# Copying the second operand of a split product with two strided transfers per pair instead of five, and swapping the high and low halves

## The chip, the cores and the metric

The kernel runs on one core of one Trainium2 chip. The metric is the device time of one execution in microseconds (us), the median over executions. Everything below that is called a span is the time from the first to the last instruction of one profiled execution; the time of an execution is a little longer than its span.

## The reference

Two stages follow each other. The first is an attention through 49 agents, for 4 batches of 12800 rows of 128 channels; the second is a gated causal convolution with 5 taps and two 128 x 128 weights.

```python
scale = 1.0 / np.sqrt(q.shape[-1])
def sm(a, b):
    s = scale * (a @ b.transpose(0, 2, 1))
    s = s - s.max(-1, keepdims=True)
    e = np.exp(s)
    return e / (e.sum(-1, keepdims=True) + 1e-09)
agent_v = sm(agents, k) @ v            # (4, 49, 128)
x = sm(q, agents) @ agent_v            # (4, 12800, 128)
xp = np.concatenate([np.zeros((B, 4, D)), x], axis=1)
gate_pre = sum(conv_w[k] * xp[:, k:k + S, :] for k in range(5))
gate = 1.0 / (1.0 + np.exp(-gate_pre))
return (gate * (x @ w_val)) @ w_out
```

## The kernel before

x is never formed. It is the product of 49 softmax weights per row with 49 vectors per batch, so the convolution and the value product are taken on the 49 weights directly, with weights folded once per batch: for each tap, and for the value, a 49 x 128 matrix.

**Split products.** Softmax weights and folded weights are each kept as a high and a low half in 16 bits. Of the product (high + low) x (high + low) three parts are kept: high x high, low x high, and high x low. The tile x1 holds, for every row of the sequence (in its columns), 128 partitions: the 49 high halves (0 to 48), the 49 low halves (49 to 97), and the first 30 of the high halves once more (98 to 127, NDUP = 30). Against it stand the folded weights: high, high again, and the low halves of the first 30. For the remaining 19 of the high x low products there is no room in 128 partitions, so a second tile, x2, takes them: it holds high rows 29 to 48 of x1 (20 rows, X2R = 20) five times over, shifted by 0 to 4 columns, one copy for each tap, in 100 partitions. One matmul over x2 then adds the missing part for all five taps.

**Units and pairs.** A batch has 10 units of 1280 rows. For every unit the scores of the queries are taken on TensorE, a softmax follows on DVE, POOL and ACT, and the weights are split into the tile pt (ACT writes the high half at L713, POOL the second copy of 30 at L718 and the low half at L726). pt is then turned into x1: for the first four units by ten transposes on TensorE (L757) and two copies (ACT L764, DVE L769), afterwards by one transposing transfer on the SP queue (L743). When a pair of units is in x1, `shifts` issues the copies into x2 (L791): five transfers, one for each tap, each of 20 partitions; for the first four units this is done for each unit by itself, and of the first unit's five transfers two are issued from ACT's queue.

**Chunks.** The convolution goes over 100 chunks of 512 columns. Each chunk takes five matmuls over x1 (L828, one for each tap) and one over x2 (L832) into the gate, a tanh on ACT (L841), one matmul over x1 (L855) and one over x2 (L859) into the value, a product on DVE (L868), a split into two 16-bit halves (ACT L874, POOL L879), three output matmuls (L898, L899, L900), a copy on ACT (L912) and, for every second chunk, a store on the SP queue (L927). The output matmuls of a chunk are placed two chunks behind its gate matmuls. In between stand the scores of later queries (L363), the keys of the next batch and its agent values (L463).

**Folding the weights.** Once per batch `fold_weights` makes the folded weights: normalisation and scales on DVE (L506 to L528), high halves (L563, L568), copies of these on ACT (L579, L583), low halves by `rest` (instructions at L548: two for the value, two for the gates), then eight transposes on TensorE (L593), and the same for the output weights (L613 to L662).

**Order.** All steps are given to a planner (`Plan`) with an estimated duration each. It keeps TensorE's steps in the order in which they were given, and orders the steps of DVE, ACT, POOL and the SP queue by the length of what depends on them, using the estimates. A step that issues a transfer carries its issue time and its time on the wire. Every engine then runs its own list in order, and waits where something is missing.

Of the kernel before, what the change touches and what calls it, by code (L numbers as in the profile page):

```python
# [13 lines left out]
ALU = mybir.AluOpType  # L14
# [8 lines left out]
UNIT = 1280  # L23
# [4 lines left out]
TAPS = 5  # L28
HALO = TAPS - 1
PAD = 16  # L30
NDUP = 30
X2LO = 29
X2R = 20


NLOAD = 11
# [135 lines left out]
def tile_agent_attention_gated_conv(  # L172
# [9 lines left out]
    nc = tc.nc  # L182
    B, C, N = qT.shape
    A = 49
# [31 lines left out]
    x1 = const.tile([P, PAD + N], F16, name="x1")  # L216
# [27 lines left out]
    def bank():  # L244
# [16 lines left out]
        out=fold, in0=ident[:, 0:AP_], in1=ident[:, AP_:P], op=ALU.add  # L261
# [217 lines left out]
    gw = const.tile([P, TAPS, A], F32, name="gw")  # L479
# [5 lines left out]
    def fold_weights(b):  # L485
        x = b % 2
        wst, unscale, oscale = wst_sb[x], unscales[x], oscales[x]
        stat, wo16 = stats[x], wo16s[x]
        dve = nc.vector
        pt, at_t = small(b)  # L490
# [14 lines left out]
        def normalise():  # L505
# [8 lines left out]
                out=gw, in0=avT.unsqueeze(1).to_broadcast([P, TAPS, A]),  # L514
                in1=conv_sb.unsqueeze(2).to_broadcast([P, TAPS, A]), op=ALU.mult,
# [4 lines left out]
        def gate_scale():  # L520
# [12 lines left out]
        pv = pv_  # L533
# [3 lines left out]
                out=pv[:, 0:A], lhsT=wval_sb, rhs=avT, start=True, stop=True  # L537
            ),
            ["avT", "moe"], [at_v], key="m",
        )  # L540
        x2g = wst[:, TAPS + 1, 0 : TAPS * X2R].rearrange("p (k r) -> p k r", k=TAPS)
        x2v = wst[:, TAPS + 2, 0 : TAPS * X2R].rearrange("p (k r) -> p k r", k=TAPS)
        ghi = wst[:, 0:TAPS, 0:A]
        vhi = wst[:, TAPS, 0:A]
        off = NDUP - X2LO

        def rest(out, full, s, hi):
            dve.scalar_tensor_tensor(  # L548
                out=out, in0=full, scalar=rs[:, s : s + 1], in1=hi,
                op0=ALU.mult, op1=ALU.subtract,  # L550
            )

        def val_weights():
            dve.tensor_reduce(
                out=mx[:, 1:2], in_=pv[:, 0:A], axis=AX.X, op=ALU.max,
                apply_absolute_value=True,
            )
            dve.tensor_scalar(
                out=mx[:, 1:2], in0=mx[:, 1:2], scalar1=TINY, scalar2=1.0 / WS,
                op0=ALU.max, op1=ALU.mult,  # L560
            )
            dve.reciprocal(out=rs[:, 1:2], in_=mx[:, 1:2])
            dve.tensor_scalar_mul(vhi, pv[:, 0:A], rs[:, 1:2])  # L563
            rest(wst[:, TAPS, 2 * A :], pv[:, 0:NDUP], 1, vhi[:, 0:NDUP])
            rest(x2v[:, HALO, off:], pv[:, NDUP:A], 1, vhi[:, NDUP:])

        def gate_weights():
            dve.tensor_scalar_mul(ghi, gw, rs[:, 0:1])  # L568

        def gate_rest():  # L570
            rest(wst[:, 0:TAPS, 2 * A :], gw[:, :, 0:NDUP], 0, ghi[:, :, 0:NDUP])
            rest(x2g[:, :, off:], gw[:, :, NDUP:], 0, ghi[:, :, NDUP:])

        w_ = ("wst", x)
        add("dve", 0.4, gate_weights, ["gw", "rsg"], [(*w_, "g")])
# [36 lines left out]
        def unscales_():  # L612
# [6 lines left out]
                out=wo, in0=wout_sb, scalar1=unscale[:, 1:2], scalar2=1.0,  # L619
# [47 lines left out]
    def queries(b, u):  # L667
        g = b * NU + u
        x = g % 2
        i = slot_of["q", b, u]  # L670
        ps, at = bank()
        sT, d, e, w, r, sm = sts[x], qw[g % 3], qw[g % 3], qw[g % 3], qr[x], qsm[x]
        pt = pts[g % 3]
        sa = sT[:, :, 0:A]
        add("pe", 1.07, lambda: score_matmuls(b, ld[i], ps), [("ld", i)], [at], key="sc")
        add("dve", 0.84, lambda: transpose_blocks(sT, ps[:, :, 0:GT]), [at], [("sT", x)])
        add(
            "dve", 0.62,
            lambda: nc.vector.tensor_reduce(out=qmx[x], in_=sa, axis=AX.X, op=ALU.max),  # L679
            [("sT", x)], [("qmx", x)],  # L680
        )
        add(
            "pool", 1.05,
            lambda: nc.gpsimd.tensor_tensor(  # L684
                out=d, in0=sa, in1=qmx[x].unsqueeze(2).to_broadcast([P, NBLK, A]),
                op=ALU.subtract,
            ),
            [("sT", x), ("qmx", x)], [("qw", g % 3)],
        )
        add(  # L690
            "act", 0.6,
            lambda: nc.scalar.activation(out=e, in_=d, func=AF.Exp, scale=SCALE),
            [("qw", g % 3)], [("qw", g % 3)],
        )

        def sums():
            nc.vector.tensor_reduce(out=sm, in_=e, axis=AX.X, op=ALU.add)
            nc.vector.scalar_tensor_tensor(
                out=sm, in0=sm, scalar=1.0 / QS, in1=tiny, op0=ALU.mult, op1=ALU.add
            )  # L700
            nc.vector.reciprocal(out=r, in_=sm)

        add("dve", 0.95, sums, [("qw", g % 3)], [("qr", x)])
        add(
            "dve", 0.68,
            lambda: nc.vector.tensor_tensor(
                out=w, in0=e, in1=r.unsqueeze(2).to_broadcast([P, NBLK, A]), op=ALU.mult
            ),
            [("qw", g % 3), ("qr", x)], [("qw", g % 3)],
        )  # L710
        p_ = ("pt", g % 3)
        add(
            "act", 0.58, lambda: nc.scalar.copy(out=pt[:, :, 0:A], in_=w),  # L713
            [("qw", g % 3)], [(*p_, 0)],
        )
        add(
            "pool", 0.44,
            lambda: nc.gpsimd.tensor_scalar(  # L718
                out=pt[:, :, 2 * A :], in0=w[:, :, 0:NDUP], scalar1=1.0, scalar2=0.0,
                op0=ALU.mult, op1=ALU.add,  # L720
            ),
            [("qw", g % 3)], [(*p_, 2)],
        )
        add(
            "pool", 1.09,
            lambda: nc.gpsimd.tensor_tensor(  # L726
                out=pt[:, :, A : 2 * A], in0=w, in1=pt[:, :, 0:A], op=ALU.subtract
            ),
            [("qw", g % 3), (*p_, 0)], [(*p_, 1)],
        )  # L730
# [43 lines left out]
    def shifts(b, u):  # L774

        g = b * NU + u
        if g >= SINGLE and g % 2 == 0:
            return
        n = 1 if g < SINGLE else 2
        u0 = u + 1 - n  # L780
        s = g // 2
        x2 = x2s[s % 3]
        o = (g + 1 - n) % 2 * UNIT
        src = [(x, v) for v in range(max(u0 - 1, 0), u + 1) for x in ("x1", "x1b")]
        for k in range(TAPS):
            c = PAD - HALO + u0 * UNIT + k

            q, e = (nc.scalar, "act") if g == 0 and k % 2 else (nc.sync, "dma")
            add(
                e, 0.75,  # L790
                lambda k=k, c=c, q=q: q.dma_start(  # L791
                    out=x2[k * X2R : (k + 1) * X2R, o : o + n * UNIT],
                    in_=x1[X2LO : X2LO + X2R, c : c + n * UNIT],
                ),
                src, [("x2", s % 3, o + i * UNIT, k) for i in range(n)], 0.26 * n,
            )


# [4 lines left out]
    def gates(t):  # L803
        b, n0, w = chunks[t]
        x = b % 2
        stat, unscale = stats[x], unscales[x]
        if t < NT:
            banks[t] = gate[:, 0:w], "gate", val[:, 0:w], "val"
        else:
            ps, at = bank()  # L810
            banks[t] = ps[:, 0, 0:w], at, ps[:, 1, 0:w], (*at, 1)
        pg, at_g = banks[t][:2]
        units = sorted({max(n0 - HALO, 0) // UNIT, (n0 + w - 1) // UNIT})
        seg = (b * NU + units[-1]) // 2
        halves = sorted({(b * NU + n // UNIT) % 2 * UNIT for n in (n0, n0 + w - 1)})
        segs_ = sorted({(b * NU + n // UNIT) // 2 for n in (n0, n0 + w - 1)})
        assert len(segs_) == 1
        x2 = x2s[segs_[0] % 3]
        o2 = n0 - (segs_[0] * SEG - b * N)
        xs = [("x1", u) for u in units] + [("x1b", u) for u in units]  # L820
        x2k = [("x2", segs_[0] % 3, h, k) for h in halves for k in range(TAPS)]
        st = [("stat", x, 0), ("stat", x, 1)]
        scale = w / CH

        def matmuls():
            for k in range(TAPS):
                c = PAD - HALO + n0 + k
                nc.tensor.matmul(  # L828
                    out=pg, lhsT=stat[:, k, :], rhs=x1[:, c : c + w],
                    start=(k == 0), stop=False,  # L830
                )
            nc.tensor.matmul(  # L832
                out=pg, lhsT=stat[0 : TAPS * X2R, TAPS + 1, :],
                rhs=x2[0 : TAPS * X2R, o2 : o2 + w], start=False, stop=True,
            )

        th = ths[t % NT_][:, 0:w]
        add("pe", 1.3 * scale, matmuls, xs + x2k + st, [at_g], key="c")
        add(
            "act", 0.16 + 0.46 * scale,  # L840
            lambda: nc.scalar.activation(out=th, in_=pg, func=AF.Tanh, scale=unscale[:, 0:1]),  # L841
            [at_g, ("unscale", x)], [("th", t % NT_)],
        )
        return stat, x2, o2, xs, x2k, st, th
# [117 lines left out]
    for b in range(B):  # L962
        t0 = b * NCH
        for i in range(NU):
            g = b * NU + i + LEAD
# [92 lines left out]
```

## Time and profile before

| | |
|---|---|
| median of 3 runs | 432.69 us (429.56 to 434.14) |
| the profiled execution: time, span | 431.22 us, 429.4 us |
| TensorE (PE) busy | 402.9 us, 94% of the span |
| ACT, DVE, POOL busy | 300.4, 297.0, 224.3 us |
| granted TensorE clock, mean | 0.996 |
| DMA | 128.07 MB, mean 298 GB/s |
| transfers into x2 | 108 on the SP queue, 2 on ACT's |

The profile comes from one execution. Engines are PE (matmul), PEld (weight load, beside PE), DVE, ACT, POOL and SP; a name with q behind it is the queue in which an engine's instructions stand. L828 is line 828 of the kernel. In the profile a tile is named without its number, so x1 and x2 are both "x", and a transfer from x1 to x2 is written x<-x. A group of instructions has its busy time, the mean duration of one, the idle time of the engine just ahead of it and what ended that idle time.

### The profile page before, as it was taken

To read this page: it belongs to the slowest core of one execution; us is meant where nothing else is said; L and a number is where in the kernel's file an instruction comes from. 1 tells how busy PE (TensorE), PEld (TensorE's weight loads), DVE (VectorE), ACT (ScalarE), POOL (GpSimd) and SP (SyncE) were. 2 spreads that over 40 slices of the span, in tenths; PEclk is the share of its full clock that TensorE was granted. 3 is DMA by queue.
4 is the path that set the end of the run, shared out by engine and by line. 5 is a ranking of instruction groups with operands and counts; after the bars stand their busy time and mean duration, and the time that the engine had idled before them with its cause. 6 is when DMAs were issued, how large, how long until landed. Compare 5 with 4: busy or idle time off the path is not lost.

```text
span 429.4 us, 8968 instructions
## 1 busy us (share of the span) xinstructions
PE 402.9 (94%) x3307; PEld 194.8 (45%) x3307; DVE 297.0 (69%) x555; ACT 300.4 (70%) x520; POOL 224.3 (52%) x239
## 2 busy tenths in 40 slices
PE   3978888999999999999999999999999999999995
PEld 1357333345565444444555544445555544434443
DVE  3776879886786877578666887678666787566231
ACT  1464536678976577778876676778876577777875
POOL 1002246564466665544557665553356466687553
PEclk9999989999999999999999999999999999999999
DMA  8999999999999999999999999999999999887743
GB/s 288 422 415 415 371 350 337 297 285 309 343 358 294 249 270 289 307 309 305 340 329 356 292 323 292 320 312 334 306 330 257 289 291 287 215 199 173 192 156 122
DMA packets 76158, 128.07 MB, mean 298 GB/s; under 512 B 51644, under 2 KB 51900, under 8 KB 76116
## 3 DMA queue, kind: packets, MB, share of 16 engines
q1 hardware_dynamic: 76056, 127.41, 96.0%
q8 instruction: 26, 0.43, 0.4%
q14 instruction: 16, 0.13, 0.1%
q10 hardware_dynamic: 60, 0.10, 0.1%
HBM read 79.25 MB, written 26.21 MB: 246 GB/s over the span
## 4 chain that ended last, share of the span: by engine, by line
PE 65%; DMA 13%; DVE 12%; ACT 5%; issue 3%; SPq 1%; POOL 1%; DVEq 0%; ACTq 0%; POOLq 0%
PE gate L828 20%; PE sc L363 13%; PE av L463 6%; PE gate L832 4%; PE val L855 4%; PE val L859 4%; PE out L898 4%; PE out L899 4%; PE out L900 4%; DMA ld<-qT 3%; DMA ld<-vP 3%; DVE h L868 2%; ACT e L455 2%; DMA ld<-kT 2%; DMA outT<-ob 2%
## 5 line engine op out<-in xcount | busy, mean ns | idle before, releaser
L879 POOL TENSOR_TENSOR hl<-h,hh 128x512 f16<-128x512 f32 (+1 forms) x101 | 117.0, 1160 | 121.3 <-ACT hh L874 113.7
L828 PE MATMUL gate<-x,stat 128*128 128x512 f16 (+1 forms) x500 | 124.4, 378 | 2.4 <-ACT th L841 2.3
L868 DVE SCALAR_TENSOR_TENSOR h<-th,val 128x512 f32<-128x512 f32 x100 | 67.7, 677 | 69.1 <-PE out L899 46.1
L363 PE MATMUL sc<-ld,ag_sb 128*32 128x320 f32 x1280 | 102.0, 452 | 10.0 <-DMA ld<-kT 8.0
L912 ACT ACTIVATE ob<-out,oscale 128x512 f32<-128x512 f32 x98 | 67.2, 686 | 23.5 <-PE out L900 17.4
L841 ACT ACTIVATE th<-gate,unscale 128x512 f32<-128x512 f32 x100 | 68.3, 683 | 19.7 <-PE gate L832 18.0
L828 PEld LDWEIGHTS <-stat 128*128 128x128 f16 x505 | 45.6, 97 | 66.4 <-issue 19.0
L874 ACT CAST hh<-h 128x512 f16<-128x512 f32 (+1 forms) x101 | 61.4, 608 | 13.1 <-DVE h L868 12.4
L684 POOL TENSOR_TENSOR qw<-sT,qmx 128x490 f32<-128x490 f32 x40 | 41.5, 1038 | 50.2 <-DVE qmx L679 50.1
L363 PEld LDWEIGHTS sc<-ld,ag_sb 128*32 128x32 f32 x1280 | 37.0, 112 | 62.8 <-issue 22.5
L463 PE MATMUL av<-ld,eT 128*64 128x129 f32 x800 | 49.5, 275 | 1.7 <-DMA ld<-vP 1.4
L389 ACT COPY ks<-sc 128x640 f32<-128x640 f32 x40 | 27.7, 691 | 32.7 <-PE sc L363 30.6
L463 PEld LDWEIGHTS av<-ld,eT 128*64 128x64 f32 x800 | 43.7, 136 | 11.7 <-issue 7.3
L726 POOL TENSOR_TENSOR pt<-qw,pt 128x490 f16<-128x490 f32 x40 | 44.7, 1119 | 3.8 <-ACT pt L713 3.1
L455 ACT ACTIVATE e<-ks,kbias 128x320 f32<-128x320 f32 x80 | 39.0, 553 | 6.1 <-DVE kbias L444 3.3
L373 DVE STREAM_TRANSPOSE eT<-e 128x640 f32<-128x640 f32 x40 | 33.6, 842 | 11.4 <-ACT e L455 5.9
L373 DVE STREAM_TRANSPOSE sT<-sc 128x640 f32<-128x640 f32 x40 | 33.3, 834 | 10.8 <-PE sc L363 10.6
L398 DVE TENSOR_REDUCE kmx<-ks 128x2 f32<-128x640 f32 x39 | 31.4, 817 | 11.8 <-ACT ks L389 11.8
L832 PE MATMUL gate<-x,stat 100*128 100x512 f16 x100 | 38.0, 380 | 0.8 <-DMA x<-x 0.8
L855 PE MATMUL val<-x,stat 128*128 128x512 f16 x100 | 37.8, 378 | 0.1
L859 PE MATMUL val<-x,stat 100*128 100x512 f16 x100 | 37.8, 378 | 0.0
L898 PE MATMUL out<-hh,wo 128*128 128x512 f16 x98 | 37.1, 379 | 0.0
(125 smaller groups left out, 392.1 us busy)
## 6 DMA issues: line engine op xcount, KB each, us to landing
ld<-vP SPq DMA_DIRECT2D x40, 645.0 KB
ld<-kT SPq DMA_DIRECT2D x40, 640.0 KB
ld<-qT SPq DMA_DIRECT2D x40, 640.0 KB
outT<-ob SPq DMA_DIRECT2D x48, 512.0 KB
x<-x SPq DMA_DIRECT2D x90, 100.0 KB
x<-x SPq DMA_DIRECT2D x18, 50.0 KB
outT<-ob SPq DMA_DIRECT2D x3, 256.0 KB
x<-pt SPq DMA_TRANSPOSE x36
```

Of the source, the lines that this page charges most:

```text
L363: nc.tensor.matmul(out=out[g * BLK : (g + 1) * BLK, j, 0:GT], lhsT=ag_sb[:, b, j * BLK : (j + 1) * BLK], rhs=src[:, g * GT : (g + 1) * GT] ...
L373: nc.vector.transpose(out=out.rearrange("p n (j i) -> p j n i", j=2), in_=in_.rearrange("p j (n i) -> p j n i", i=BLK),)
L463: nc.tensor.matmul(out=av[o : o + AP_, 0 : C + 1], lhsT=et[:, n, :], rhs=vt[:, n, :], start=(u == 0 and n < 2), stop=(u == NU - 1 and n >= ...
L828: nc.tensor.matmul(out=pg, lhsT=stat[:, k, :], rhs=x1[:, c : c + w], start=(k == 0), stop=False,)
L832: nc.tensor.matmul(out=pg, lhsT=stat[0 : TAPS * X2R, TAPS + 1, :], rhs=x2[0 : TAPS * X2R, o2 : o2 + w], start=False, stop=True,)
L841: lambda: nc.scalar.activation(out=th, in_=pg, func=AF.Tanh, scale=unscale[:, 0:1]),
L855: nc.tensor.matmul(out=pv, lhsT=stat[:, TAPS, :], rhs=x1[:, PAD + n0 : PAD + n0 + w], start=True, stop=False,)
L859: nc.tensor.matmul(out=pv, lhsT=stat[0 : TAPS * X2R, TAPS + 2, :], rhs=x2[0 : TAPS * X2R, o2 : o2 + w], start=False, stop=True,)
L868: lambda: nc.vector.scalar_tensor_tensor(out=h, in0=th, scalar=1.0, in1=pv, op0=ALU.add, op1=ALU.mult),
L874: "act", 0.16 + 0.42 * scale, lambda: nc.scalar.copy(out=hh, in_=h),
L879: lambda: nc.gpsimd.tensor_tensor(out=hl, in0=h, in1=hh, op=ALU.subtract),
L912: lambda: nc.scalar.activation(out=ob[:, o : o + w], in_=po, func=AF.Copy, scale=oscale),
```

## The change

The 19 rows that x2 needs are now copied by two transfers, each with all five taps: one takes 15 rows from every third partition, the other takes four neighbouring rows. Each row of the source is read five times, at five column offsets, and lands in five neighbouring partitions of x2. x2 is thus ordered by row and, within a row, by tap; it has 95 partitions instead of 100. So that every third row of the first 45 is the one that goes to x2, the second copy in x1 now takes the other two of every three. High and low halves change places in x1: the low halves lie in partitions 0 to 48, the high halves in 49 to 97. The rows that are copied lie in partitions 51, 54, ... 93 and 94 to 97. In `fold_weights` the low halves go to the matching places, by three instructions instead of two for the value and four instead of two for the gates. All copies into x2 are issued from the SP queue.

```diff
-NDUP = 30
-X2LO = 29
-X2R = 20
+THREES = 15
+NDUP = 2 * THREES
+X2R = 19
+X2CUTS = ((0, THREES, 3, 0.5), (THREES, X2R, 1, 0.3))
...
-        x2g = wst[:, TAPS + 1, 0 : TAPS * X2R].rearrange("p (k r) -> p k r", k=TAPS)
+        x2g = wst[:, TAPS + 1, 0 : TAPS * X2R].rearrange("p (r k) -> p k r", k=TAPS)
...
-            rest(wst[:, TAPS, 2 * A :], pv[:, 0:NDUP], 1, vhi[:, 0:NDUP])
-            rest(x2v[:, HALO, off:], pv[:, NDUP:A], 1, vhi[:, NDUP:])
+            pv3, hi3 = threes(pv[:, 0:A]), threes(vhi)
+            rest(
+                wst[:, TAPS, 2 * A :].rearrange("p (i r) -> p i r", r=2),
+                pv3[:, :, 0:2], 1, hi3[:, :, 0:2],
+            )
+            rest(x2v[:, HALO, 0:THREES], pv3[:, :, 2], 1, hi3[:, :, 2])
+            rest(x2v[:, HALO, THREES:], pv[:, 3 * THREES : A], 1, vhi[:, 3 * THREES :])
...
-            rest(wst[:, 0:TAPS, 2 * A :], gw[:, :, 0:NDUP], 0, ghi[:, :, 0:NDUP])
-            rest(x2g[:, :, off:], gw[:, :, NDUP:], 0, ghi[:, :, NDUP:])
+            gw3, hi3 = threes(gw), threes(ghi)
+            twos = wst[:, 0:TAPS, 2 * A :].rearrange("p k (i r) -> p k i r", r=2)
+            for r in range(2):
+                rest(twos[:, :, :, r], gw3[:, :, :, r], 0, hi3[:, :, :, r])
+            rest(x2g[:, :, 0:THREES], gw3[:, :, :, 2], 0, hi3[:, :, :, 2])
+            rest(x2g[:, :, THREES:], gw[:, :, 3 * THREES :], 0, ghi[:, :, 3 * THREES :])
...
-            "act", 0.58, lambda: nc.scalar.copy(out=pt[:, :, 0:A], in_=w),
+            "act", 0.58, lambda: nc.scalar.copy(out=pt[:, :, A : 2 * A], in_=w),
...
-                out=pt[:, :, 2 * A :], in0=w[:, :, 0:NDUP], scalar1=1.0, scalar2=0.0,
+                out=pt[:, :, 2 * A :].rearrange("p n (i r) -> p n i r", r=2),
+                in0=w[:, :, 0 : 3 * THREES].rearrange("p n (i r) -> p n i r", r=3)[:, :, :, 0:2],
+                scalar1=1.0, scalar2=0.0,
...
-                out=pt[:, :, A : 2 * A], in0=w, in1=pt[:, :, 0:A], op=ALU.subtract
+                out=pt[:, :, 0:A], in0=w, in1=pt[:, :, A : 2 * A], op=ALU.subtract
...
-        for k in range(TAPS):
-            c = PAD - HALO + u0 * UNIT + k
-            q, e = (nc.scalar, "act") if g == 0 and k % 2 else (nc.sync, "dma")
+        c = PAD - HALO + u0 * UNIT
+        for r0, r1, every, us in X2CUTS:
+            first = A + (2 if every == 3 else 3 * THREES)
+            rows = x1[first : first + 1 + (r1 - r0 - 1) * every : every, c : c + 1]
+            view = [rows.ap[0], (1, TAPS), (1, n * UNIT)]
             add(
-                e, 0.75,
-                lambda k=k, c=c, q=q: q.dma_start(
-                    out=x2[k * X2R : (k + 1) * X2R, o : o + n * UNIT],
-                    in_=x1[X2LO : X2LO + X2R, c : c + n * UNIT],
+                "dma", 0.6,
+                lambda r0=r0, r1=r1, rows=rows, view=view: nc.sync.dma_start(
+                    out=x2[r0 * TAPS : r1 * TAPS, o : o + n * UNIT],
+                    in_=bass.AP(rows.tensor, rows.offset, view),
                 ),
-                src, [("x2", s % 3, o + i * UNIT, k) for i in range(n)], 0.26 * n,
+                src, [("x2", s % 3, o + i * UNIT, r0) for i in range(n)], us * n,
             )
...
-        x2k = [("x2", segs_[0] % 3, h, k) for h in halves for k in range(TAPS)]
+        x2k = [("x2", segs_[0] % 3, h, c[0]) for h in halves for c in X2CUTS]
```

More of the change, by code (lines that the diff above doesn't have):

```diff
@@ L540, in fold_weights, with threes @@
         )
-        x2g = wst[:, TAPS + 1, 0 : TAPS * X2R].rearrange("p (k r) -> p k r", k=TAPS)
-        x2v = wst[:, TAPS + 2, 0 : TAPS * X2R].rearrange("p (k r) -> p k r", k=TAPS)
+        x2g = wst[:, TAPS + 1, 0 : TAPS * X2R].rearrange("p (r k) -> p k r", k=TAPS)
+        x2v = wst[:, TAPS + 2, 0 : TAPS * X2R].rearrange("p (r k) -> p k r", k=TAPS)
         ghi = wst[:, 0:TAPS, 0:A]
         vhi = wst[:, TAPS, 0:A]
-        off = NDUP - X2LO
+        def threes(x):
+            if len(x.shape) == 2:
+                return x[:, 0 : 3 * THREES].rearrange("p (i r) -> p i r", r=3)
+            return x[:, :, 0 : 3 * THREES].rearrange("p k (i r) -> p k i r", r=3)
         def rest(out, full, s, hi):
```

## The prediction

> **What bounds the kernel now.** I read the page first, then the busy time in four stretches, then TensorE's own waits, and only then the chain at the one place where x2 is late.
>
> ```profile
> span 429.4 us, 8968 instructions
> PE 402.9 (94%) x3307; PEld 194.8 (45%) x3307; DVE 297.0 (69%) x555; ACT 300.4 (70%) x520; POOL 224.3 (52%) x239
> DMA  8999999999999999999999999999999999887743
> GB/s 288 422 415 415 371 350 337 297 285 309 343 358 294 249 270 289 307 309 305 340 329 356 292 323 292 320 312 334 306 330 257 289 291 287 215 199 173 192 156 122
> ```
>
> TensorE is busy for 402.9 of 429.4 us; 26.5 us are left in the whole span. The DMA engines look full as well (9 in nearly every slice), so the page alone leaves two candidates: TensorE, or transfers that TensorE waits for. The stretches tell them apart (columns: length, then busy time of PE, PEld, DVE, ACT, POOL, granted clock, DMA share, GB/s).
>
> ```profile
> 0.00:40.00 40.00, 28.50 (x366) 16.64 (x368) 25.69 (x50) 18.84 (x34) 4.20 (x13) 1.00 0.96 383
> 40.00:100.00 60.00, 54.05 (x493) 23.97 (x495) 48.97 (x101) 36.79 (x63) 29.45 (x34) 0.97 1.01 332
> 100.00:420.00 320.00, 315.55 (x2425) 151.53 (x2422) 220.81 (x402) 239.65 (x415) 187.54 (x190) 1.00 0.98 286
> 57.00:58.00 1.00, 1.00 (x13) 0.23 (x8) 0.49 (x1) 0.88 (x2) 0.41 (x1) 0.61 1.04 430
> 58.00:60.00 2.00, 2.00 (x20) 0.67 (x16) 1.80 (x5) 0.11 (x2) 0.00 (x0) 0.50 1.00 415
> 60.00:61.00 1.00, 1.00 (x7) 0.32 (x4) 1.00 (x2) 0.56 (x1) 0.80 (x2) 0.68 0.99 407
> ```
>
> From 100 to 420 us TensorE idles 320.00 - 315.55 = 4.5 us: whatever the transfers do there, no more than that is to be had. From 40 to 100 it idles 6.0 us, and the last three rows show a piece of it, from about 57.2 to 60.6 (0.61 and 0.68 are the edges), in which the granted clock was 0.50. Ahead of 40 us nothing is copied into x2 yet. Now TensorE's waits (engine, line, who ended it: us in total, times, longest):
>
> ```profile
> PE sc L363 <- DMA ld<-kT: 8.0, 4, 7.1
> PE gate L828 <- ACT th L841: 2.3, 6, 0.7
> PE val L655 <- DVE wsp L642: 1.9, 1, 1.9
> PE sc L363 <- DVE sT L373: 1.9, 3, 0.8
> PE av L463 <- DMA ld<-vP: 1.4, 5, 0.4
> PE sc L757 <- POOL pt L726: 1.2, 1, 1.2
> PE gate L593 <- DVE wst L548: 1.1, 1, 1.1
> PE gate L832 <- DMA x<-x: 0.8, 1, 0.8
> PE av L629 <- ACT stat L608: 0.3, 1, 0.3
> ```
>
> This is the view that decides. Of all of TensorE's waits one belongs to x2, and it is 0.8 us long. The waits for loads belong to the start (the longest, 7.1 us, is the first load of all). What remains is DVE, ACT and POOL handing over late, most of it around the folding of the weights.
>
> **The change, part by part.** *Five transfers become two.* The single late copy, in the chain that ended last:
>
> ```profile
> 325.44 7.18 DMA x<-pt
> ...
> 332.69 0.76 SPq L791
> ...
> 335.02 0.71 SPq L791
> ...
> 335.77 5.16 DMA x<-x
> ```
>
> The transposed unit lands at 332.6, then five issues of 0.71 to 0.76 us follow one another on the SP queue, and the last lands 5.16 us after its issue at 335.77, at 340.9; TensorE had been ready 0.8 us before. With two issues the last one leaves at 332.69 + 0.76 = 333.5 and lands, at the same 5.16 us, at 338.6. The wait goes: **-0.8 us**. What is late next there is nothing, since TensorE's own work is then the last to arrive by 1.7 us. An issue of the new kind isn't in the trace; it lies between an issue of today (0.71) and the nearest larger one on this queue, the transposing transfer with a median of 2.8 us. At 2.8 the second would leave at 335.5 and land at 340.7, and 0.4 of the 0.8 would stay. I take 0.75, since it is the same plain copy. In the other places the copies are early enough already, so 2.2 us less of SP time per pair buy nothing: loads and stores behind them leave sooner, and TensorE doesn't wait for either after the first 40 us.
>
> ```profile
> L791 ACTq DMA_DIRECT2D x<-x x2: 719/1020/1321, 41.2 to 42.6; - x2
> 43.37 0.61 ACT L692 ACTIVATE qw<-qw 128x490 f32<-128x490 f32 x1 [2.68 <-DMA x<-x]
> 42.50 0.29 DVE L491 COPY av<-av 128x129 f32<-128x129 f32 x1 [1.29 <-PE av L463]
> ```
>
> *Two issues leave ACT's queue.* At 41.2 us ACT issues two copies (0.72 and 1.32 us), and the exponential of the second query unit behind them starts only at 43.37. Without them it can start about 2.0 us sooner, and the sums that DVE makes of it can fall into DVE's idle 1.29 us ahead of 42.50. Between 0 and -2.1 us; DVE's next work is the first folding, which I expect to take part of the gain back, so **-0.6 us**, about half of that idle time. On the SP queue two issues stand where three stood, so this step passes nothing there.
>
> *Three more DVE instructions per folding.*
>
> ```profile
> 46.61 0.39 DVE L548 SCALAR_TENSOR_TENSOR wst<-val,rs,wst 128x30 f16<-128x30 f32 x2
> 46.92 0.60 DVE L548 SCALAR_TENSOR_TENSOR wst<-gw,rs,wst 128x150 f16<-128x150 f32 x2
> 147.59 0.39 DVE L548 SCALAR_TENSOR_TENSOR wst<-av,rs,wst 128x30 f16<-128x30 f32 x2
> 148.66 1.05 DVE L548 SCALAR_TENSOR_TENSOR wst<-gw,rs,wst 128x150 f16<-128x150 f32 x2
> 148.79 1.28 PE L363 MATMUL sc<-ld,ag_sb 128*32 128x320 f32 x16 [0.79 <-DVE sT L373]
> 347.67 1.60 DVE L548 SCALAR_TENSOR_TENSOR wst<-gw,rs,wst 128x150 f16<-128x150 f32 x2
> 347.99 1.17 POOL L726 TENSOR_TENSOR pt<-qw,pt 128x490 f16<-128x490 f32 x1
> ```
>
> Two instructions over 49 elements take 0.39 us, two over 245 take 0.60: (0.60 - 0.39) / 196 = 1.07 ns an element, and (0.39 - 49 x 0.00107) / 2 = 0.17 us for each instruction beside its elements. The elements stay the same, three instructions come, so +0.51 us per folding: 0.17 for the value, 0.34 for the gates. In the first folding all of it stands ahead of the transposes for which TensorE waits (1.1 us at L593): +0.5. In the second and third the value's part stands ahead of the transpose of scores for which TensorE waits 0.79; the gates' part falls behind it, into DVE's slack: +0.2 each. In the fourth DVE carries the chain from the gates' part through to the copies for which TensorE waits 0.3: +0.5. Together **+1.4 us**. From below the bound is 0 (DVE has 31% idle). From above it is set by the fourth folding's row, where the same two took 1.60 instead of 0.60 with a POOL instruction beside them: 4 x 0.51 + 3 x 1.0 = +5.0. I stay near the undisturbed rows, since in the first two foldings the pair took 0.60 and 1.05.
>
> [...]
>
> *The second copy of the high half takes two of every three.*
>
> ```profile
> L718 POOL TENSOR_SCALAR pt<-qw 128x300 f16<-128x300 f32 x40 | 17.6, 441 | 17.5 <-DVE qw L706 16.2 <-PE gate L828 1.1 <-DMA x<-pt 0.2
> L726 POOL TENSOR_TENSOR pt<-qw,pt 128x490 f16<-128x490 f32 x40 | 44.7, 1119 | 3.8 <-ACT pt L713 3.1
> L879 POOL TENSOR_TENSOR hl<-h,hh 128x512 f16<-128x512 f32 (+1 forms) x101 | 117.0, 1160 | 121.3 <-ACT hh L874 113.7
> 64.00:92.00 28.00, 25.66 (x221) 10.24 (x217) 25.07 (x42) 19.22 (x33) 18.06 (x20) 1.00 1.02 325
> ```
>
> The same 300 elements, in runs of two. I take 0.44 as before: **0**. From above, L726's 1.12 us: 0.68 more, 40 times. Behind 92 us POOL's 121.3 us of idle ahead of L879 hide that. From 64 to 92, where DVE is busy 25.07 of 28 and POOL 18.06, L718 stands five times: at most 5 x 0.68 = +3.4.
>
> *The rest is free.* ACT and POOL write the same elements to other columns of pt. The matmuls over x2 have 95 rows instead of 100, which takes no less time:
>
> ```profile
> L832 PE MATMUL gate<-x,stat 100*128 100x512 f16 x100 | 38.0, 380 | 0.8 <-DMA x<-x 0.8
> L855 PE MATMUL val<-x,stat 128*128 128x512 f16 x100 | 37.8, 378 | 0.1
> ```
>
> TensorE's order is as the work was listed, so the new estimates can only shift steps on DVE, ACT, POOL and SP; I give that no sign. No wait is added.
>
> **The sum**: -0.8 - 0.6 + 1.4 + 0 = 0.0 on the profiled execution's 431.2 us (its span of 429.4 and 1.8 around it). That execution lies 1.5 below the median of the runs shown, 432.7, and two of the three runs are longer than it. I predict a little above the sum: **431.5 us**.
>
> **The rivals.** *Everything early comes out well.* ACT's two issues bring the full -2.1, the foldings' instructions hide, the late copy goes (-0.8), and the half-speed stretch of 3.4 us (57.2 to 60.6) doesn't come back because TensorE's waits ahead of it shrink: -1.7. Together -4.6: 426.6 us. For it: DVE is the late engine from 40 to 92 us, and the sums would leave it earlier. Against it: the 1.9 us wait at L655 ahead of that stretch hangs on DVE's folding, which gets longer.
>
> *POOL gets into DVE's way.* The copy in runs of two rises to 1.12 (+3.4 from 64 to 92), and the instructions of the later three foldings are each held by a POOL instruction once more (+3.0): 437.6 us. It decides from about 0.8 us for L718 together with L548 groups above 1.6. Against it: L718's input has gaps already (30 of every 49).
>
> *The transfers don't arrive sooner.* [...] Then the 0.8 us wait stays: 432.0 us.
>
> [...]
>
> **How the numbers follow.** Forecast 0.60 (429 to 434), early gains 0.20, POOL in the way 0.10, no sooner 0.10. About 1% is what a measurement of this kernel tells from no change: faster is below 428.4, slower above 437.0. The early rival lies below 428.4; forecast and the last rival are within; POOL's is above. So 0.2, 0.7, 0.1. The range leaves out half of the early rival and most of POOL's: 426.5 to 436.0; the upper ends of the folding and of L718 are not expected together.
>
> **What would show it.** Right: no wait of L832 for x<-x; 44 transfers into x2 instead of 110, two issues below 1 us each; the queue of ACT gone from the list; 28 instructions at L548 instead of 16, L593's wait 0.5 longer; TensorE's busy time within 1 us of 402.9. Wrong: L718 well above 0.44; transfers of x2 that land later than 6 us behind their issue; a clock of 0.5 at another place or not at all; or TensorE's idle time from 100 to 420 far from 4 us, which would mean that the order on the other engines changed more than I allow.

## The result and the profile after

The changed kernel takes **444.01 us** (median of 4 executions, 443.26 to 445.90); the kernel before took 432.81 beside it. The ratio is 1.0277, with an interval of 1.0212 to 1.0342. It is slower, and outside the predicted range.

The page of the kernel after, first the span and the engines, then the granted clock in 40 slices:

```profile
span 442.1 us, 8846 instructions
...
PE 406.5 (92%) x3307; PEld 195.4 (44%) x3307; DVE 298.9 (68%) x567; ACT 300.0 (68%) x520; POOL 225.4 (51%) x239
...
PEclk9989999999999999969999999989999999999999
```

The span grew by 442.1 - 429.4 = 12.7 us. TensorE is busy 3.6 us longer with the same number of matmuls, and idle 442.1 - 406.5 = 35.6 us instead of 26.5, so 9.1 longer: together the 12.7. Two slices in the middle with a clock below 0.9 (the 6 and the 8 behind it) say where most of the 3.6 are. The stretches (length, busy time of PE, PEld, DVE, ACT, POOL, granted clock, DMA share, GB/s):

```profile
40.00:100.00 60.00, 52.47 (x489) 23.20 (x487) 49.51 (x103) 36.47 (x63) 29.28 (x34) 1.00 1.01 331
100.00:420.00 320.00, 307.82 (x2372) 147.21 (x2369) 218.70 (x407) 229.57 (x400) 182.62 (x185) 0.98 0.94 279
186.00:189.00 3.00, 0.11 (x1) 0.10 (x1) 2.22 (x4) 1.95 (x5) 1.62 (x2) 0.84 1.08 363
189.00:192.00 3.00, 3.00 (x8) 1.06 (x7) 1.65 (x4) 1.33 (x3) 0.92 (x1) 0.50 0.98 405
192.00:195.00 3.00, 3.00 (x17) 0.88 (x18) 0.69 (x1) 2.08 (x4) 1.73 (x3) 0.53 1.06 343
293.00:297.00 4.00, 2.55 (x7) 0.88 (x7) 2.35 (x6) 2.38 (x4) 0.90 (x2) 0.60 1.06 386
```

From 100 to 420 TensorE idles 12.2 us, where it idled 4.5; from 40 to 100 it idles 7.5 instead of 6.0. Around 188 it stands still for about 3 us, and then runs at half clock for 6 us; around 294 it stands still as long, and the half clock lasts about 3 us. The waits name the cause (engine, line, who ended it: us in total, times, longest), first those of the engines, then the SP queue's own:

```profile
ACT ob L933 <- DMA outT<-ob: 10.3, 2, 5.4
PE gate L849 <- ACT th L862: 9.9, 8, 3.1
...
ACT pt L731 <- DMA x<-pt: 4.4, 1, 4.4
...
PE gate L611 <- DVE wst L557: 1.5, 1, 1.5
```

```profile
SPq L763 <- DMA x<-x: 40.2, 10, 6.3
```

The same waits of before:

```profile
ACT ob L912 <- DMA outT<-ob: 4.1, 2, 2.5
...
SPq L743 <- DMA x<-x: 0.9, 3, 0.5
```

TensorE waits for the tanh of ACT (9.9 instead of 2.3 us), ACT waits for an output buffer to be stored (two times, 5.4 us at the longest), and on the SP queue there is a wait that was not there: the transposing transfer (L763) waits ten times for a copy into x2. The transfer writes a unit of x1 that no copy is reading. In the compiled program fourteen transposing transfers wait for a 15-row copy that stands two to six places ahead of them on the queue, and in all fourteen the columns that the copy reads and those that the transfer writes don't overlap. The trace shows eight semaphores that the queue's transfers use in turn (31 or 32 of the 255 transfers each), so a transfer can also have to wait for the one eight places ahead of it, whatever that is. In the program of before, twenty transposing transfers wait for a copy, all of them in this way; its 0.9 us may belong to them. Only the fourteen are new. The program's dependency tracking draws them where the source takes every third partition: with neighbouring partitions (the run neighbours, below) they are gone.

The chain that ended last, cut to 175 to 189 us, and under it the first matmuls behind it from TensorE's timeline with the idle time ahead of them in brackets:

```profile
175.77 0.70 ACT th L862
...
176.49 7.64 DMA outT<-ob
...
184.22 0.09 ACT ob L933
...
188.17 0.68 ACT th L862
```

```profile
188.89 2.29 PE L849 MATMUL gate<-x,stat 128*128 128x512 f16 x5 [3.12 <-ACT th L862]
...
294.45 2.29 PE L849 MATMUL gate<-x,stat 128*128 128x512 f16 x5 [3.13 <-ACT th L862]
```

A store issued at 176.49 lands 7.64 us later; ACT, which needs its buffer, stands still until then; what follows on ACT and, in between, on POOL is late with it, and the tanh ends at 188.85; TensorE idles 3.12 us, and its next five matmuls take 2.29 us at the granted clock of 0.50 in the row of 189 to 192 above. Why did the store leave so late? Its data are there at 166.75, when this copy on ACT ends:

```profile
166.06 0.69 ACT L933 ACTIVATE ob<-out,oscale 128x512 f32<-128x512 f32 x1 [0.34 <-PE out L921]
```

The SP queue of the kernel after in these microseconds (start, duration, what is issued):

```profile
168.11 1.65 SPq L812 DMA_DIRECT2D x<-x  x2
169.87 2.39 SPq L361 DMA_DIRECT2D ld<-kT  x2
174.29 1.48 SPq L763 DMA_TRANSPOSE x<-pt  x1
...
176.49 0.38 SPq L948 DMA_DIRECT2D outT<-ob  x1
```

Between 172.26 and 174.29 the queue stands still: the transposing transfer waits 2.0 us for the copies issued at 168.11. The store stands behind it and leaves 9.7 us after its data. In the queue of the kernel before the same store and the one behind it stand ahead of this transfer:

```profile
170.22 0.34 SPq L927 DMA_DIRECT2D outT<-ob  x1
...
171.97 0.34 SPq L927 DMA_DIRECT2D outT<-ob  x1
172.64 8.12 SPq L743 DMA_TRANSPOSE x<-pt  x2
```

There the store leaves 5.5 us after its data, and ACT doesn't wait for it.

Why this store? A batch has 25 chunks, a buffer takes two, and the last chunk of a batch takes one by itself. So the buffer ahead of that single one (the batch's twelfth) comes round again after three chunks, where most come round after four. Both long waits of ACT, 5.4 us up to 184.22 and 5.0 up to 289.77, are for the store of the twelfth buffer, in the first batch and in the second, which leave 9.7 and 8.8 us after their data. Other stores of the kernel before leave up to 12 us after theirs, and ACT waits little for them (4.1 us in all).

The planner orders the queue by its estimates, and the new ones put the transfer in front of the stores. So the change brought two things that its diff doesn't show: **a wait, and a new place in the queue for what stands behind it.** The experiments take them apart.

### The profile page after: what moved, and what is told of

Its sections match the earlier page's. It is cut to its first block, busy times and chain, and to the rows that moved or that the text cites. A ratio compares the mean times of both kernels' runs of the same rounds, so it can differ in the third digit from the quotient of the medians.

```text
span 442.1 us, 8846 instructions
## 1 busy us (share of the span) xinstructions
PE 406.5 (92%) x3307; PEld 195.4 (44%) x3307; DVE 298.9 (68%) x567; ACT 300.0 (68%) x520; POOL 225.4 (51%) x239
## 4 chain that ended last, share of the span: by engine, by line
PE 60%; DMA 14%; DVE 13%; ACT 6%; issue 3%; POOL 2%; SPq 1%; DVEq 0%; ACTq 0%; POOLq 0%
PE gate L849 19%; PE sc L366 11%; PE av L466 7%; PE val L876 4%; PE gate L853 4%; PE val L880 4%; PE out L919 4%; PE out L920 4%; DMA outT<-ob 4%; PE out L921 3%; DMA ld<-qT 3%; DMA x<-pt 3%; DMA ld<-vP 3%; DVE h L889 3%; ACT e L458 2%
## 5 line engine op out<-in xcount | busy, mean ns | idle before, releaser
L849 PE MATMUL gate<-x,stat 128*128 128x512 f16 (+1 forms) x500 | 126.3, 383 | 9.9 <-ACT th L862 9.9
L746 POOL TENSOR_TENSOR pt<-qw,pt 128x490 f16<-128x490 f32 x40 | 44.5, 1115 | 13.0 <-ACT pt L731 12.7
L466 PEld LDWEIGHTS av<-ld,eT 128*64 128x64 f32 x800 | 43.7, 136 | 10.3 <-issue 7.2
L376 DVE STREAM_TRANSPOSE sT<-sc 128x640 f32<-128x640 f32 x40 | 33.3, 835 | 12.5 <-PE sc L366 12.3
L853 PE MATMUL gate<-x,stat 95*128 95x512 f16 x100 | 38.5, 385 | 0.0
L880 PE MATMUL val<-x,stat 95*128 95x512 f16 x100 | 38.1, 381 | 0.0
```

Of the source, the lines that this page charges most:

```text
L376: nc.vector.transpose(out=out.rearrange("p n (j i) -> p j n i", j=2), in_=in_.rearrange("p j (n i) -> p j n i", i=BLK),)
L466: nc.tensor.matmul(out=av[o : o + AP_, 0 : C + 1], lhsT=et[:, n, :], rhs=vt[:, n, :], start=(u == 0 and n < 2), stop=(u == NU - 1 and n >= ...
L849: nc.tensor.matmul(out=pg, lhsT=stat[:, k, :], rhs=x1[:, c : c + w], start=(k == 0), stop=False,)
L853: nc.tensor.matmul(out=pg, lhsT=stat[0 : TAPS * X2R, TAPS + 1, :], rhs=x2[0 : TAPS * X2R, o2 : o2 + w], start=False, stop=True,)
L880: nc.tensor.matmul(out=pv, lhsT=stat[0 : TAPS * X2R, TAPS + 2, :], rhs=x2[0 : TAPS * X2R, o2 : o2 + w], start=False, stop=True,)
```

## The experiments

All times are medians; ratios are against the kernel before on the same chip.

**nowait: the changed kernel in its own order, without the fourteen waits.** The transposing transfer is declared independent of the copies whose columns it doesn't write.

```diff
+                it = nc.sync.dma_start_transpose(...)
+                for copy, first_cut, cb, lo, hi in copied:
+                    if first_cut and not lo - 1 <= u <= hi:
+                        tc.declare_no_dep(it.ins, copy.ins, reason="other columns of x1")
```

> The changed kernel with its own order on every queue; only the 14 waits of a transposing transfer for the 15-row copy of an earlier pair are gone (the transfer writes other columns of x1 than that copy reads). Theory A, the new wait holds the SP queue: time falls from 444 to 430-434 us, the transposing transfers' 40 us of waiting for x<-x disappear, and TensorE's waits for the tanh (9.9 us) fall to about 2-3. Theory B, the planner's new estimates put the steps in a worse order: it stays at 440-446. Theory C, the two new copies or the longer folding cost it: it stays at 440-446 too.

431.26 us, ratio 1.0001 (0.9973 to 1.0029). The stretch from 100 to 420 and TensorE's wait, then the SP queue at the place shown above:

```profile
100.00:420.00 320.00, 315.58 (x2439) 152.20 (x2432) 222.81 (x413) 239.57 (x417) 188.04 (x190) 1.00 0.96 283
```

```profile
PE gate L856 <- ACT th L869: 2.8, 6, 0.7
```

```profile
161.62 1.64 SPq L819 DMA_DIRECT2D x<-x  x2
163.36 2.84 SPq L361 DMA_DIRECT2D ld<-kT  x2
166.25 3.10 SPq L764 DMA_TRANSPOSE x<-pt  x1
...
170.07 0.37 SPq L955 DMA_DIRECT2D outT<-ob  x1
```

The queue holds the same things in the same order. The transfer leaves as soon as the loads ahead of it are issued, and the same store leaves at 170.07 instead of 176.49. Of the 6.4 us between them, the copies were 6.5 us late already (168.11 against 161.62), which I put down to the waits of earlier pairs (between 140 and 170 us the transposing transfers of the changed kernel wait 9.5 us for copies, in two waits); the wait adds 2.0, and shorter issues of the loads and the transfer (2.39 and 1.48 against 2.84 and 3.10) take 2.1 back. All of the loss is gone with the waits, so the folding's instructions, the 15/4 rows and the copy in runs of two cost nothing that can be measured.

**oldorder: the waits stay, the order is that of before.** The planner is given the five old copies as steps; two of them issue the new transfers, three issue nothing.

```diff
+        at_ = (0, 2) if g == 0 else (0, 1)
+        for k in range(TAPS):
+            e = "act" if g == 0 and k % 2 else "dma"
             add(
-                "dma", 0.6,
+                e, 0.75,
+                (lambda i=at_.index(k): copy(i)) if k in at_ else (lambda: None),
```

> The changed kernel, but the planner is given the five copies' estimates of the kernel before (three of the five steps issue nothing), so that every engine has the order of before; the 14 waits stay. Theory A: still slow, 438-446 us, with 30-40 us of the transposing transfers waiting for x<-x. Theory B: 430-434. Theory C: 440-446.

431.15 us, ratio 1.0009 (0.9989 to 1.0030).

```profile
SPq L763 <- DMA x<-x: 50.1, 12, 9.1
...
PE gate L855 <- ACT th L868: 2.4, 6, 0.7
```

The waits are there, longer than in the changed kernel, and harmless. That is against the expectation of theory A, which had named the wait alone. In this kernel neither the wait nor the order costs anything measurable by itself: the loss takes both.

**oldorder_nowait: both undone.**

> Order of before and no such waits; the two copies, the swap and the longer folding stay. Theories A and B alone or together: 430-434 us. Theory C: 438-446. The prediction's sum for just this (copies, ACT's queue, folding) was 431.

430.83 us, ratio 0.9999 (0.9979 to 1.0020). With both undone the new copies bring no gain: the 0.8 us wait for x2 is gone, and that is less than can be told from nothing. No version ran measurably faster than the kernel before.

**before_wait: the kernel before, with the wait put in.** Each transposing transfer waits for the last of the five copies issued ahead of it.

```diff
+                for copy in copied[-1:]:
+                    tc.add_manual_dep(it.ins, copy.ins.name, ..., reason="wait")
```

> The kernel before with one thing added: each transposing transfer waits until the last of the five copies issued before it has landed (15 waits are left in the program). Theory A: 438-446 us, the SP queue waits 30-60 us there, and TensorE waits for the tanh for 8 us or more. Theories B and C: 431-435.

446.45 us, ratio 1.0372 (1.0337 to 1.0407).

```profile
SPq L744 <- DMA x<-x: 37.7, 14, 6.0
...
ACT ob L922 <- DMA outT<-ob: 15.1, 6, 4.6
...
PE gate L838 <- ACT th L851: 10.2, 11, 4.3
```

Without any of the change's other parts the wait brings the same chain of stalls. It also shows that the order of before is no safe one: with five issues and the wait for the last of them it loses more than the changed kernel.

**stores_first: the changed kernel with its waits, the stores moved ahead of the waiting transfer.** Where the planner had put stores behind the first transposing transfer after a pair of copies, and ahead of the next transfer or copy, this transfer goes behind the last of them that the order allows; loads that stand between move ahead with the stores.

```diff
-    for i in plan.order():
+    order = plan.order()
+    ...
+            order = order[:p] + order[p + 1 : q + 1] + [i] + order[q + 1 :]
```

> The changed kernel with its waits (13 left); only on the SP queue, where a transposing transfer that comes first behind the copies into x2 has stores behind it, it is put behind those stores instead. Theory A2, the wait costs time by holding the stores that stand behind it, so that the ring of output buffers runs out and ACT stops: 430-435 us, 30-50 us of waiting for x<-x still there, ACT's wait for a store 2-4 us as in the kernel before. Rival A3, the wait costs because the transposed unit itself comes late or because loads come late: 438-446, as the transposing transfers get later still.

432.52 us, ratio 1.0026 (0.9996 to 1.0056).

```profile
SPq L763 <- DMA x<-x: 25.5, 7, 6.1
...
ACT ob L933 <- DMA outT<-ob: 0.6, 1, 0.6
...
PE gate L849 <- ACT th L862: 2.1, 5, 0.7
```

The transfer still waits seven times, up to 6.1 us, in sum 25.5 us where 30 to 50 were expected; ACT's wait for an output buffer falls from 10.3 to 0.6, and nearly all of the loss is gone. oldorder has shown that twice as much waiting is harmless, so the shorter sum isn't the reason: what cost the time is what stood behind the waiting transfer.

**ring4: a fourth output buffer**, order and waits as in the changed kernel.

```diff
-    obs = ring(NOB, [P, 2 * CH], F32, "ob")
+    obs = ring(NOB + 1, [P, 2 * CH], F32, "ob")
-    ob = obs[pair % NOB]
+    ob = obs[pair % (NOB + 1)]
```

> The changed kernel, its order and its waits; four output buffers stand in turn instead of three, while the planner goes on with three, so that no step changes place. A2: ACT no longer stops for a store (10.3 us of that wait gone), so 431-435 us, with at most the 1.6 us left where ACT waits for a transposing transfer at 132 us. A3: 440-446.

440.69 us, ratio 1.0222 (1.0171 to 1.0272), where 431 to 435 were expected.

```profile
ACT pt L731 <- DMA x<-pt: 12.6, 3, 6.9
...
PE gate L849 <- ACT th L862: 8.8, 9, 4.1
...
ACT ob L933 <- DMA outT<-ob: 3.2, 2, 1.6
```

ACT waits less for output buffers, but now for pt, which the late transposing transfer hasn't read. So the ring of output buffers is one of two doors by which a late SP queue reaches ACT.

**stores_late and stores_late_nowait: the order of before with the stores moved behind the transfer**, with the waits and without them. It was meant as the mirror of stores_first: a store (j) that stands between a pair's copies and the transfer (i) goes behind the transfer.

```diff
-    for i in plan.order():
+    order = plan.order()
+    ...
+                order = order[:p] + order[p + 1 : q + 1] + [j] + order[q + 1 :]
```

> The changed kernel in the order of the kernel before (431.15 with its 12-14 waits in place), and now the stores that stood between the copies into x2 and the waiting transposing transfer are put behind that transfer (16 waits). A2: slower again, 438-448 us, with ACT waiting 10 us or more for stores. A3: 430-434, since the transposed units come earlier, not later.

> The order of the five-copy estimates with the stores moved behind the transposing transfer that follows the copies, and no transposing transfer waits for a copy: the stores are issued in the same late place as in the run before, but nothing ahead of them on SP's queue waits for a landing. A (the wait with stores behind it costs the time, a late place in the list alone does not): 430 to 433 us, no SP wait of L763 for x<-x, ACT's wait for an output buffer under 5 us in sum. B (a late place of the stores costs the time by itself, since each transfer ahead of them holds the queue for 1 to 5 us): 438 to 442 us, as with the waits.

440.92 us, ratio 1.0226 (1.0160 to 1.0293), and 439.11, ratio 1.0165 (1.0125 to 1.0206). The second speaks against the strict form of my theory, by which a late place costs nothing without the wait for a copy. The waits of the second:

```profile
SPq L764 <- POOL pt L746: 49.1, 9, 9.4
...
ACT ob L946 <- DMA outT<-ob: 9.6, 3, 4.7
...
PE gate L862 <- ACT th L875: 6.9, 7, 2.4
```

The edit went further than the changed kernel's order: it put two or three stores in a row behind a transfer, in six places with two of them the other way round, and there the transfer waits for POOL's low half, up to 9.4 us. In this order a store behind the transfer took over whatever the transfer waited for. The false wait is one such thing; here another was enough.

**oldorder_five and oldorder_nowait_five: three more issues per pair.** before_wait loses 15 us and oldorder nothing, both in the order of before. One difference is the five issues. Here three small transfers (20 rows of 128 B, into partitions of x2 that nobody reads) follow the two copies.

```diff
+        def small(k):
+            nc.sync.dma_start(
+                out=x2[100:120, o + 64 * k : o + 64 * k + 64],
+                in_=x1[29:49, c : c + 64],
+            )
```

> The changed kernel in the order of before, with the waits of the transposing transfers for the copies, and with three more issues per pair behind the two copies on SP's queue (20 rows of 128 B each into partitions of x2 that nobody reads), so that a pair costs five issues again. Queue theory (what decides is how late SP's queue gets the stores out; the two copies save about 2.2 us of issues per pair, and that is why the order of before bears the waits with two copies, 431.15, and not with five, 446.45): 437 to 447 us, TensorE's wait for a tanh above 6 us in sum, ACT's wait for an output buffer above 6. Wait theory (with five copies the wait was for the last of them, which lands later; issues alone cost nothing): 430 to 433 us.

> The same three more issues per pair in the order of before, without the waits. Both theories: 430 to 433 us, since before issues five copies too, without waits, in 431 to 432 us. Above 436 it would mean that the small transfers cost by themselves, and the run beside it could not be read.

432.68 us, ratio 1.0056 (1.0030 to 1.0083), and 431.50, ratio 1.0003 (0.9978 to 1.0027). Three more issues by themselves are no explanation, and together with the waits they cost about 2 us, not 15. But the extra issues also cover part of the copy's landing: the waits are 10.4 us in sum here. So five issues with waits as long as those of before_wait were not tried, and the 15 us of before_wait stay unexplained. It waits for the last of five copies, this run for the first of two.

**Open in part:** which of the waits starts a stall. The sum of the waits doesn't order the times (50.1 us in oldorder are harmless, 37.7 in before_wait and 40.2 in the changed kernel are not). For the two long stalls of the changed kernel, the lateness of the twelfth buffer's store says more. In oldorder it leaves 0.6 and 1.5 us after its data in the first two batches, and ACT waits for neither; in stores_first 3.8 and 4.9, and ACT waits 0.6 us for the first; in nowait 4.3 and 4.4, and ACT waits 2.3 us for the second; in the changed kernel 9.7 and 8.8, and ACT waits 5.4 and 5.0. In before_wait it leaves after 5.7 and 6.9 us, and ACT waits only 1.7 us for the first: most of its loss lies elsewhere and wasn't followed. Nor is lateness all of it: in nowait ACT waits behind 4.4 us of it and in the kernel before not behind 5.5, so how long the store takes to land counts too.

**neighbours: the 15 rows from neighbouring partitions.** The rows stand at 79 to 93, the second copy takes the first 30 as before, the folding has its old instructions, and no transposing transfer waits for a copy.

```diff
-X2CUTS = ((0, THREES, 3, 0.5), (THREES, X2R, 1, 0.3))
+X2CUTS = ((0, THREES, 1, 0.5), (THREES, X2R, 1, 0.3))
-            first = A + (2 if every == 3 else 3 * THREES)
+            first = A + NDUP + r0
```

> The changed kernel and its order, two copies and the swap of halves, but the 15 rows are neighbours (partitions 79 to 93) instead of every third, the second copy of the high half is the first 30 rows again, and the folding has its two and two instructions as before. No transposing transfer waits for a copy then. Theory A (the wait comes from the step between partitions): 429-433 us; about 0.5-1.5 below the version without waits, as the folding is shorter. If the two copies themselves are what costs, 438-446.

455.63 us, ratio 1.0528 (1.0446 to 1.0610). That was a miss: taking the stride away takes the wait away, and yet this is the slowest kernel of all. Waits, then a piece of the chain:

```profile
PE gate L843 <- DMA x<-x: 2.7, 3, 1.8
...
ACT ob L923 <- DMA outT<-ob: 23.5, 6, 8.8
```

```profile
135.09 7.61 DMA x<-x
```

TensorE waits for x2 again, and the copy in the chain lands 7.61 us after its issue, where the late one of before took 5.16. The twelfth buffer's stores leave 11.3 and 12.3 us after their data, and ACT waits 6.3 and 8.8 us for them. That slower copies make the stores late is likely, but this run alone doesn't show it.

**alone: the copies by themselves.** Behind the end of the changed kernel each kind of copy is issued twice, each waiting for the one before.

```diff
+    def alone(first, every, count):
+        rows = x1[first : first + 1 + (count - 1) * every : every, PAD : PAD + 1]
+        view = [rows.ap[0], (1, TAPS), (1, SEG)]
+        nc.sync.dma_start(out=x2s[0][0 : count * TAPS, :], in_=bass.AP(rows.tensor, rows.offset, view))
```

> The changed kernel, with eighteen copies behind its end whose results nobody reads (the output is complete before them): the five copies of 20 rows from partitions 29 to 48, then one copy of 75 rows from every third partition 51 to 93, one from the adjacent partitions 79 to 93, one from the adjacent 29 to 43, one from every second partition 65 to 93, and one of 20 rows from four partitions; all twice, each kind waiting for the one before, on an otherwise idle chip. Source-partition theory (copies out of adjacent partitions are slow in themselves): the adjacent 79 to 93 and 29 to 43 land at least 1.3 times as long after their issue as every third. Row-count theory (75 rows over 16 engines, whichever partitions): all 75-row copies within 10% of each other. Traffic theory (the adjacent copy was late only because of what ran beside it): the same as row count, here without other traffic. The time of the whole is about 30 us above the changed kernel's and says nothing.

The whole took 500.95 us.

The second turn on the SP queue, in this order: 15 partitions every third from 51, adjacent from 79, adjacent from 29, every second from 65, and the four-partition copy. From one issue to the next is the time of one copy:

```profile
474.05 0.88 SPq L1039 DMA_DIRECT2D x<-x  x1
...
478.02 0.89 SPq L1039 DMA_DIRECT2D x<-x  x1
...
484.00 0.85 SPq L1039 DMA_DIRECT2D x<-x  x1
...
490.08 0.86 SPq L1039 DMA_DIRECT2D x<-x  x1
...
494.11 0.70 SPq L1039 DMA_DIRECT2D x<-x  x1
```

3.97 us for every third, 5.98 and 6.08 for adjacent partitions, 4.03 for every second. The same 75 rows of 5 KB into the same 75 partitions take half as long again when the 15 source partitions are neighbours. This is what the source-partition theory forecast; row count and traffic are out.

## Why the prediction was wrong, by its own steps

**The step that failed** stands just before the sum: "I give that no sign. No wait is added." The first half left out that the estimates were part of the change: with two short steps in place of five, the planner moved the transposing transfer ahead of stores. The second half was taken from the code's own dependencies, where no step of the transfer names a copy. It should have been asked of the compiled program's dependency tracking, which drew fourteen waits here: the transfer writes x1, a copy reads x1, and this copy reads it by a stride over partitions. Together the two were worth +12.7 us of span (one alone costs nothing measurable: 431.15 and 431.26), and neither had a term or a rival. A wait on the SP queue, with the stores behind it named, leads to ACT's output buffers and from there to the tanh for which TensorE already waited 2.3 us before.

**"2.2 us less of SP time per pair buy nothing"** held in oldorder_nowait (430.83).

**The late copy of x2, -0.8:** the wait went as forecast. No wait of L853 for x<-x is left, and two issues take 1.65 us together. That 0.8 us were gained is not shown; it is less than the runs can tell.

**ACT's two issues, -0.6, and the folding, +1.4:** the wait at L611 is 1.5 where it was 1.1, so +0.4 of the +0.5 that I took for the first folding. The instructions of the folding grew by 1.6 us in all (the rows of this line add up to 7.5 us after and 5.9 before), so 0.40 per folding where 0.51 was forecast. What ACT's queue and the later foldings gave or took can't be told apart: their sum was near zero, and nowait lies at 1.0001. **The copy in runs of two, 0:** right.

```profile
L736 POOL TENSOR_SCALAR pt<-qw 128x300 f16<-128x300 f32 x40 | 17.9, 448 | 17.5 <-DVE qw L724 15.3 <-PE gate L849 1.1 <-DMA x<-pt 1.1
L557 DVE SCALAR_TENSOR_TENSOR wst<-gw,rs,wst 128x75 f16<-128x75 f32 (+1 forms) x16 | 5.4, 427 | 0.0
```

448 ns instead of 441, and a mean of 427 ns for a gate instruction of the folding. In each of the later three foldings one gate instruction beside POOL's L746 took longer, 0.63, 0.62 and 1.13 us; before, beside L726, it took 0.82, 0.83 and 1.15. So POOL got no further into DVE's way, which was my only rival above 437.0 us.

**"TensorE's busy time within 1 us of 402.9":** wrong by 3.6, most of it the half clock behind the new stops, at 188 to 195 and 294 to 297 us; the half clock of before, from 57.2 to 60.6, didn't come back (1.00 there), though the wait at L655 ahead of it, now at L673, was 1.92 us in both kernels; that shorter waits would take it away is shown by no run. So the sign "a clock of 0.5 at another place" came too. The last sign I named ("idle time from 100 to 420 far from 4 us, which would mean that the order on the other engines changed more than I allow") is what came: 12.2 us. I had named it as a sign and given it no case of its own, so the range ended at 436.0.

**What the sum without the hidden part gives:** 431.2 to 431.5 forecast, 431.26 measured once the waits are taken out. The listed terms add up to what was measured; since they cancel to nearly zero, that is no test of each of them. The missing ones decided.

## What to carry to other kernels

When a copy's access pattern changes, ask of every later writer of the source whether the dependency tracking can still tell the two apart; here a stride of three over partitions brought fourteen waits and neighbouring partitions none, and the waits appeared on an instruction that the diff doesn't touch. Where a planner orders queues by estimates, changed estimates are a change of the order: list the queue before and after, and look at what now stands behind an instruction that can wait. A store in a queue can get onto the critical path when its buffer comes round again: here ACT waited 5.4 and 5.0 us for two of them.

## What the runs showed of the hardware that was not expected

**Copies out of neighbouring source partitions took longer.** 5.98 and 6.08 us against 3.97 for every third partition and 4.03 for every second, above, with the same number of rows and bytes. Why they took longer is shown by no run. The prediction had no term for the partitions that a copy reads; the stride of three that brought the false wait also kept the copy at 3.97 us.

**Behind two stops of 3.1 us the clock was halved.** Behind TensorE's 3.12 us of idling up to 188.89 the granted clock was 0.50 from 189 to 192 us and 0.53 up to 195, so half of some 6 us more was lost. Behind the 3.13 us up to 294.45 the half clock lasted only some 3 us (0.50 from 294 to 297, 1.00 from 298), so the length of these stops alone doesn't say what follows. The stops of nowait from 100 to 420 us, 0.9 us at the longest, were followed by no such piece (granted clock 1.00). In between it went both ways: 1.92 us of idling up to 55.4 us were followed by the half clock in the kernel before (0.50 from 58 to 60), and the same 1.92 us up to 55.7 were not in the changed one (1.00 from 40 to 100).
